# Softmax weights in PSUM, one sum of each unit on GpSimd, and shared PSUM banks in a fused local-attention and mixer kernel

## The chip, the cores and the metric

The kernel runs on one core of a Trainium2 chip. A core has five engines that work beside each other, each through its own queue in order: TensorE (PE, matmuls; PEld is its weight loads), VectorE (DVE), ScalarE (ACT), GpSimd (POOL) and SyncE (SP), which here issues all DMA transfers. SBUF is the working memory; PSUM, where matmuls put their results, has eight banks of 128 x 512 fp32. The metric is device time in microseconds (us), the median of several runs.

## The reference

For x of 2048 tokens by 512 channels:

```python
xn = layernorm(x)
q, k, v = split(xn @ wqkv)           # 32 heads of 16
# each position looks at itself and 7 earlier ones, 2 apart
logits = einsum(q, k[pos - 2 * r]) * 16 ** -0.5      # r = 0..7, masked before the start
s = (einsum(softmax(logits), v[pos - 2 * r])) @ wo
y = layernorm(xn)
g = silu(gelu(y @ w1 + b1) @ w2 + b2)                # 512 -> 1376 -> 512
out = x + s * g
```

## The kernel before, in words

Tokens are laid out as 128 partitions by 16; with a dilation of 2 the even and the odd tokens are two independent halves (c = 0, 1) of 8 tiles each. Attention is cut into 8 *units*, numbered u: (c = 0, 1) x (4 groups of 8 heads). Matrix products are made in fp16 with the operands split into a high and a low half, three matmuls for one.

For a unit, `qkv` makes 8 tiles of q, k, v with 12 matmuls of 384 columns each (L632); ScalarE evacuates each tile to the buffer `U` (L648), of which there are two, and DMAs make the shifted copies of k and v at the partitions' edges (`HALO`, L657). `attention` then works on DVE: four products of q with two shifts of k each (L691), each followed by a reduction over the 16 channels of a head (L694), the softmax over 8 positions (L714 to L721, with the exponential on ScalarE, L717), four products of the weights with two shifts of v each (`pv`, L747), and sums of these. The products are 128 x 2048 fp32 and live in the ring `R_prod` of three buffers. In units 0 to 6 DVE adds the second and third product to the first (`addto`, L742); what is left, three half-wide sums, is done on GpSimd during the next unit (`beside`, L771), each behind a one-element copy (L770) that makes it start when a certain product of DVE is done, so that it runs while DVE reduces. Unit 7 has no next one and sums on DVE. `emit_o` scales and splits the result (ScalarE L730, DVE L732) and a DMA transposes it into `oT` (L735).

The mixer's two layers are 4 chunks (`ch`) of 512 tokens, each with 11 steps f. `mlp1` makes 12 matmuls of 512 columns (L900), then ScalarE applies gelu in place (L917) and writes the high half h (L920). The low half is made in one of two ways, chosen by `DVE_LO`: DVE subtracts (L923), or PE subtracts h by a matmul with a negative diagonal (L929) and ScalarE writes the rest (L932). Steps 0 to 7 of the first chunk take the second way. `mlp2` (L945) adds 12 matmuls into four banks `z`, two steps later. After 11 steps ScalarE evacuates these with silu (L961, L956). The output projection `wo` (L817) runs for the first half of the tokens in `wo_first`, and at the end for the second half in `wo_last`, where the matmuls of the last unit's heads come last.

PSUM before: two banks `ps` (attention's tiles, wo), two banks `mh` (first layer), four banks `z`.

The order on every engine is not written out by hand. Each operation is entered in a plan with an engine, an estimated duration, a priority and its reads and writes; `issue` places them one after the other, always the one that can start first and among these the most urgent, and gives out ring buffers and banks as they come free in the plan. `port=True` tells the plan that a DVE and a GpSimd operation may not run beside each other. A change of a duration, a ring or a flag therefore reorders all queues. On the chip, every engine runs its list in the order planned and waits on semaphores.

The subtraction, as an example of an entry (L922 to L925): it is entered with the urgency of the first layer, ahead of attention's products, but in its queue it waits for the instruction before it like any other.

Of the kernel before, what the change touches and what calls it, by code (L numbers as in the profile page):

```python
# [8 lines left out]
F32 = mybir.dt.float32  # L9
# [4 lines left out]
ALU = mybir.AluOpType  # L14
# [4 lines left out]
P = 128  # L19
# [31 lines left out]

BEFORE_W1 = (0, 1, 4, 5)

DVE_LO = range(8, 44)


class Buf:
# [233 lines left out]
def tile_mixer(ctx, tc, a_x, a_wqkv, a_wo, b_w1, b_b1, b_w2, out):  # L291
# [18 lines left out]
    def dve(n, fn, r, w, f=1.0, port=True, c=0.065, **k):  # L310
        pl.add("dve", c + n * DVE1 * f, fn, r, w, port=port, **k)
# [45 lines left out]
    R_s = Ring(sb, [P, 8], F32, 10, "s")  # L357
    R_w = Ring(sb, [P, 16], F32, 8, "lw")
    R_bn = Ring(sb, [P, 6], F32, 4, "bn")
    R_ps = Ring(psum, [P, 512], F32, 2, "ps")  # L360
    R_mh = Ring(psum, [P, 512], F32, 2, "mh")
    R_z = [Ring(psum, [P, 512], F32, 1, f"z{i}") for i in range(4)]

    def f32v(t, k):
# [246 lines left out]
    def qkv(c, hb, u):  # L611
        ub = u % 2
        U3 = U[ub].rearrange("p (s e) -> p s e", e=P)
        cs = R_cs.new()
        act(NI, lambda: nc.scalar.activation(cs.t, cT[:, c], AF.Identity, scale=qsc[:, hb, 1:2]),
            [("c", c, i) for i in range(NI)] + [("qi", hb)], [cs], prio=PEV) if u else [
            dve(len(g), lambda q=cpos[g[0]], n=len(g), g=g: nc.vector.tensor_scalar(
                cs.t[:, q:q + n], cT[:, c, q:q + n], 1.0 / YS if g[0] in FP else qsc[:, hb, 1:2], None, op0=ALU.mult),
                [("c", c, i) for i in g] + ([] if g[0] in FP else [("qi", hb)]), [(cs, g)], prio=0.15)
            for g in groups]  # L620
        cp = lambda i: cpos[i] if c == 0 else i
        csk = {i: (cs, g) for g in groups for i in g} if u == 0 else {i: cs for i in range(NI)}
        for n, i in enumerate(IORD if u else IORD0):
            more = n % 2 and (u == 0 or u == 1 and n < U1MH)
            y = yT[c * 2 + i // 4]
            o = (i % 4) * P
            b = (R_mh if more else R_ps).new()

            def mm(n0=0, n1=12, y=y, o=o, b=b):
                for n in range(n0, n1):  # L630
                    (s, t), k = ((0, 0), (1, 0), (0, 1))[n // KT], n % KT
                    nc.tensor.matmul(b.t[:, 0:384], y[:, s, k, o:o + P], wq[:, hb, t, k],  # L632
                                     start=(n == 0), stop=(n == 11))

            ends = [4, 8, 12] if u < 2 else [12]
            if u == 0 and i in FP:
                yf = yF[i]
                for k in range(KT):
                    pe(1, 384, lambda k=k, b=b, yf=yf: nc.tensor.matmul(
                        b.t[:, 0:384], yf.t[:, k * P:(k + 1) * P], stq[hb]()[:, k * 384:(k + 1) * 384],  # L640
                        start=(k == 0), stop=(k == KT - 1)), [yf, ("stq", hb, k)], [b], fp32=4.1,
                       holds=stkey[hb], after=pl.users([b] + [("v", ub, i)]))
                ends = []
            for n0, n1 in zip([0] + ends, ends):
                pe(n1 - n0, 384, lambda mm=mm, n0=n0, n1=n1: mm(n0, n1), [("yh" if n1 <= 4 else "y", c, i)] +
                   [("wq" if n1 == 12 else "wqh", hb, k) for k in range(min(n1, KT))], [b],
                   after=pl.users([b] + [("v", ub, i)]))
            act(384, lambda i=i, b=b: nc.scalar.activation(  # L648
                U3[:, i:i + 31:15, :], b.t[:, 0:384].rearrange("p (t e) -> p t e", t=3),
                AF.Identity, scale=cs.t[:, cp(i):cp(i) + 1]), [b, csk[i], ("kz", ub)],  # L650
                [("q", ub, i), ("k", ub, i), ("v", ub, i)], prio=PEV)

        ks = [("k", ub, i) for i in range(1, 8)]
        vs = [("v", ub, i) for i in range(1, 8)]
        for x, h, o, src in (("k", KH, KO, ks), ("v", VH, VO, vs)):
            for n, (a, b) in enumerate(HALO):
                dma((b - a) * 3584, lambda a=a, b=b, h=h, o=o: nc.sync.dma_start(  # L657
                    U3[a:b, h:h + 7, :], U3[a - 1:b - 1, o + 1:o + 8, :]), src,
                    [(x + "h", ub, n)], rate=300e3, issue=0.6)
        vrow = v0[0:1, hb * P:(hb + 1) * P]  # L660
        if c == 0:
            dma(512, lambda: nc.sync.dma_start(vrow, U3[0:1, VO, :]), [("v", ub, 0)], [("v0", hb)])
        dma(3584, lambda: nc.sync.dma_start(
            U3[0:1, VH:VH + 7, :],
            vrow.rearrange("p (o e) -> p o e", o=1).to_broadcast([1, 7, P])),
            [("v0", hb), ("kz", ub)], [("vh0", ub)])
# [9 lines left out]
    def attention(c, hb, u):  # L676
# [35 lines left out]
        def over_r(t):  # L712
# [5 lines left out]
            table="exp", prio=PEV)  # L718
        dve(512, lambda: nc.vector.tensor_reduce(sx.t, Lt(), AX.X, ALU.add), Lk, [sx], port=False)
        dve(64, lambda: nc.vector.reciprocal(sx.t, sx.t), [sx], [sx], f=6.0, port=False)  # L720
        dve(512, lambda: nc.vector.tensor_tensor(Lt(), Lt(), over_r(sx.t), op=ALU.mult),  # L721
            [sx] + Lk, Lk)

        o16 = R_o.new()

# [18 lines left out]
        if u < 7:  # L744
            def pv(g):
                pr = R_prod.new()
                dve(2048, lambda: nc.vector.tensor_tensor(  # L747
                    pr.t.rearrange("p (r f d) -> p r f d", r=2, d=DH),
                    L3()[:, 2 * g:2 * g + 2].rearrange("p r (f o) -> p r f o", o=1)
                    .to_broadcast([P, 2, 64, DH]),  # L750
                    slots(Ut, VH, 2 * g).rearrange("p r (f d) -> p r f d", d=DH), op=ALU.mult),
                    Lk + vk + [("vh", ub, 0), ("vh", ub, 1), ("vh0", ub)], [pr])
                return pr

            def addto(a, b):
                add(2048, lambda: a.t, lambda: b.t, lambda: a.t, [a, b], a)
            acc = pv(0)
            p1 = pv(1)
            p2 = pv(2)
            addto(acc, p1)  # L760
            p3 = pv(3)
            addto(acc, p2)
            last.append(p3)

            def beside(x, y):
                def go(pr, p=PR_U * (u + 1) + 500):
                    def fn():
                        nc.gpsimd.tensor_copy(gate, pr.t[0:1, 0:1])  # L770
                        nc.gpsimd.tensor_tensor(x.t[:, 0:1024], x.t[:, 0:1024], y(), op=ALU.add)  # L771
                    pool(2.45, fn, [acc, p3, pr], [x, ("gate",)], prio=p)
                return go

            def rest(p=PR_U * (u + 2) + 700):
                with prio(p):
                    emit_o(lambda: acc.t[:, 0:1024], [acc], 0, 2)
            pend.extend([beside(acc, lambda: acc.t[:, 1024:2048]),
                         beside(p3, lambda: p3.t[:, 1024:2048]),
                         beside(acc, lambda: p3.t[:, 0:1024]), rest])  # L780
        else:

            for h in range(2):
                m = []
                for g in range(2):
                    pr = R_prod.new()
                    b0 = Ut[:, (VH + 4 * g + 4 * h) * P:]
                    win = bass.AP(b0.tensor, b0.offset, [list(b0.ap[0]), [P, 4], [DH, 32], [1, DH]])
                    dve(2048, lambda pr=pr, g=g, h=h, win=win: nc.vector.tensor_tensor(
                        pr.t.rearrange("p (r f d) -> p r f d", r=4, d=DH),  # L790
                        L3()[:, 4 * g:4 * g + 4, 32 * h:32 * h + 32]
                        .rearrange("p r (f o) -> p r f o", o=1).to_broadcast([P, 4, 32, DH]),
                        win, op=ALU.mult), Lk + vk + [("vh", ub, 0), ("vh", ub, 1), ("vh0", ub)], [pr])
                    m.append(pr)
                x, y = m
                for n, q0, q1 in ((2048, x, y), (1024, x, x), (512, x, x)):
                    add(n, lambda n=n, x=x: x.t[:, 0:n],
                        (lambda y=y: y.t) if n == 2048 else (lambda n=n, x=x: x.t[:, n:2 * n]),
                        lambda n=n, x=x: x.t[:, 0:n], [x] + ([y] if n == 2048 else []), x)
                emit_o(lambda x=x: x.t[:, 0:512], [x], h, h + 1)  # L800
# [36 lines left out]
    gu = [U[0][:, i * D:(i + 1) * D] for i in range(NI)]  # L837

    def wo_last():
        rings = [R_ps, R_ps, R_mh, R_mh] + R_z  # L840
        tiles = []
        for i in range(NI):
            b = rings[i].new()
            pe(9, 512, wo_mm(b, i, range(NHB - 1), NHB - 1 if i < NI - 1 else NHB - 2), [("oT", hb, i // 4) for hb in range(NHB - 1)] +
               [("wo", k) for k in (0, 2)], [b], prio=PR_M * 10 + 2 * i)
            tiles.append(b)
        for i in range(4):
            dma(P * 2048, lambda i=i: nc.sync.dma_start(gu[i], gd[1, i]),
# [389 lines left out]
```

## Time and profile before

| | us |
|---|---|
| median of 3 runs (423.68 to 424.52) | 423.83 |
| span of the profiled execution, first to last instruction | 422.0 |
| PE busy | 411.2 (97%) |
| DVE busy | 392.2 (93%) |
| ACT busy | 216.7 (51%) |
| POOL busy | 82.7 (20%) |

The profile gives the span of the one execution that was profiled, and not its whole time; the median of the runs stands 1.83 us above that span. The page has the busy time of each engine, the span in 40 slices with the busy share in tenths, and the chain of work that ended last. Groups give a line, an engine, an operation, the shapes and the count, then total busy time and the mean in ns of one, then the idle time ahead of them. Timelines give start and length in us. Matmul durations overlap, since matmuls are pipelined; their pace is read from the chain or from the distance of starts.

### The profile page before, as it was taken

The page shows a single profiled execution, that of the slowest core. Times are in us where ns is not written, and L with a number is a line of the kernel's source. Part 1 is how long each engine was busy: PE and PEld are TensorE (multiplying, and loading weights), DVE is VectorE, ACT ScalarE, POOL GpSimd, SP SyncE. Part 2 cuts the span into 40 slices and gives each one's busy share as a digit, 9 for nine tenths or more (in the row PEclk, how much of TensorE's full clock was granted, in tenths as well). Part 3 has the DMA queues.
Part 4 walks back from the last instruction along what each step waited for, and adds up shares of the span by engine and source line. Part 5 has one row for each costly group of instructions (what it writes and reads, how often), then busy time and mean ns, then how long its engine had stood idle before and what let it go on. Part 6 is the DMA issues. An engine that isn't in the chain of part 4 may idle for free.

```text
span 422.0 us, 5549 instructions
## 1 busy us (share of the span) xinstructions
PE 411.2 (97%) x2103; PEld 210.2 (50%) x2103; DVE 392.2 (93%) x402; ACT 216.7 (51%) x327; POOL 82.7 (20%) x119
## 2 busy tenths in 40 slices
PE   7899999999999899999999999999999999999995
PEld 5466544445644454445544554455545554444442
DVE  5958999999999999999999999998999989999974
ACT  6799983953367355854375352234230492236400
POOL 5310200002322341102500240052002500250022
PEclk8999999999999999999999999999999999999999
DMA  8962250310164036544252023110425374007142
GB/s 295 412 233 88 82 205 2 102 49 0 30 159 149 4 90 123 125 99 52 84 153 100 2 86 50 52 64 37 136 75 176 75 217 146 2 0 204 52 135 107
DMA packets 42650, 44.83 MB, mean 106 GB/s; under 512 B 27480, under 2 KB 27920, under 8 KB 42112
## 3 DMA queue, kind: packets, MB, share of 16 engines
q1 hardware_dynamic: 42624, 44.49, 35.4%
q8 instruction: 16, 0.26, 0.3%
q14 instruction: 10, 0.08, 0.1%
HBM read 23.53 MB, written 7.34 MB: 73 GB/s over the span
## 4 chain that ended last, share of the span: by engine, by line
PE 78%; DVE 15%; ACT 2%; issue 2%; POOL 1%; DMA 1%; SPq 0%; DVEq 0%
PE z L945 23%; PE ps L632 22%; PE mh L900 22%; PE ps L817 6%; DVE w L437 2%; PE z L817 2%; DVE prod L691 2%; DVE L L694 2%; PE mh L632 1%; DVE bn L525 1%; PE mh L817 1%; POOL cT L519 1%; DMA prod<-in_A_x_dram 1%; DVE prod L747 1%; DVE prod L742 1%
## 5 line engine op out<-in xcount | busy, mean ns | idle before, releaser
L900 PE MATMUL mh<-yT,w 128*128 128x512 f16 (+1 forms) x528 | 121.3, 379 | 0.7 <-ACT h L932 0.6
L632 PE MATMUL ps<-wq,yT 128*128 128x384 f16 x684 | 115.4, 326 | 2.6 <-ACT U L648 1.6
L945 PE MATMUL z<-w,h 128*128 128x512 f16 x480 | 111.2, 379 | 0.0
L632 PEld LDWEIGHTS <-yT 128*128 128x128 f16 x744 | 72.7, 98 | 51.6 <-issue 1.8
L900 PEld LDWEIGHTS <-w 128*128 128x128 f16 (+1 forms) x528 | 52.9, 100 | 61.8 <-issue 1.3
L917 ACT ACTIVATE mh<-mh,b1T,hsc 128x512 f32<-128x512 f32 (+1 forms) x44 | 33.0, 749 | 89.0 <-PE mh L900 88.6
L945 PEld LDWEIGHTS <-h 128*128 128x128 f16 x480 | 47.0, 98 | 55.0
L691 DVE TENSOR_TENSOR prod<-U 128x2048 f32<-128x2048 f32 x32 | 73.0, 2287 | 1.3 <-DMA U<-U 0.5
L694 DVE TENSOR_REDUCE L<-prod 128x128 f32<-128x2048 f32 x32 | 72.8, 2281 | 0.3
L648 ACT ACTIVATE U<-ps,cs 128x384 f32<-128x384 f32 x58 | 33.4, 577 | 60.9 <-PE ps L632 58.7
L747 DVE TENSOR_TENSOR prod<-L,U 128x2048 f32<-128x2048 f32 x28 | 63.1, 2285 | 0.2
L770 POOL COPY gate<-prod 1x1 f32<-1x1 f32 x21 | 4.4, 210 | 222.4 <-DVE prod L691 190.6
L742 DVE TENSOR_TENSOR prod<-prod,prod 128x2048 f32<-128x2048 f32 x16 | 36.5, 2282 | 0.0
L771 POOL TENSOR_TENSOR prod<-prod 128x1024 f32<-128x1024 f32 x14 | 32.9, 2349 | 0.0
L817 PEld LDWEIGHTS <-oT 128*128 128x128 f16 x189 | 18.5, 98 | 22.2
L920 ACT ACTIVATE h<-mh,hsc 128x512 f16<-128x512 f32 x40 | 27.4, 684 | 0.9
L817 PE MATMUL ps<-wo,oT 128*128 128x512 f16 x120 | 27.2, 379 | 0.0
L923 DVE SCALAR_TENSOR_TENSOR h<-mh,hsc,h 128x512 f16<-128x512 f32 x32 | 23.7, 741 | 0.9 <-ACT h L920 0.9
L730 ACT ACTIVATE o<-prod,osc 128x1024 f16<-128x1024 f32 (+1 forms) x9 | 9.4, 1050 | 14.4 <-POOL prod L771 8.9
L771 POOL TENSOR_TENSOR prod<-prod,prod 128x1024 f32<-128x1024 f32 x7 | 16.4, 2348 | 0.0
L917 ACT ACT_TABLE_LOAD x10 | 12.8, 1283 | 0.2
L810 POOL TENSOR_TENSOR U<-U,f 128x512 f32<-128x512 f32 x4 | 5.1, 1273 | 34.1 <-DVE U L880 34.1
(159 smaller groups left out, 363.6 us busy)
## 6 DMA issues: line engine op xcount, KB each, us to landing
f<-in_A_x_dram SPq DMA_DIRECT2D x31, 256.0 KB, 3.4
U<-U SPq DMA_DIRECT2D x16, 392.0 KB, 4.1
gd<-f SPq DMA_DIRECT2D x12, 256.0 KB, 2.6
oT<-in_B_w_dram SPq DMA_DIRECT2D x2, 1024.0 KB
yT<-in_B_w_dram SPq DMA_DIRECT2D x2, 1024.0 KB, 13.1
f<-gd SPq DMA_DIRECT2D x8, 256.0 KB, 2.9
out_dram<-f SPq DMA_DIRECT2D x8, 256.0 KB, 2.1
out_dram<-U SPq DMA_DIRECT2D x7, 256.0 KB, 2.0
```

Of the source, the lines that this page charges most:

```text
L632: nc.tensor.matmul(b.t[:, 0:384], y[:, s, k, o:o + P], wq[:, hb, t, k], start=(n == 0), stop=(n == 11))
L648: act(384, lambda i=i, b=b: nc.scalar.activation(U3[:, i:i + 31:15, :], b.t[:, 0:384].rearrange("p (t e) -> p t e", t=3), AF.Identity, sca ...
L691: dve(2048, lambda p2=p2, g=g: nc.vector.tensor_tensor(p2(), q, slots(Ut, KH, 2 * g), op=ALU.mult), qk + [("kh", ub, 0), ("kh", ub, 1), (" ...
L694: dve(2048, lambda pr=pr, g=g: nc.vector.tensor_reduce(L3()[:, 2 * g:2 * g + 2], pr.t.rearrange("p (r f d) -> p r f d", r=2, d=DH), AX.X, ...
L742: dve(n, lambda: nc.vector.tensor_tensor(d(), a(), b(), op=ALU.add), keys, [dkey])
L747: dve(2048, lambda: nc.vector.tensor_tensor(pr.t.rearrange("p (r f d) -> p r f d", r=2, d=DH), L3()[:, 2 * g:2 * g + 2].rearrange("p r (f ...
L771: nc.gpsimd.tensor_tensor(x.t[:, 0:1024], x.t[:, 0:1024], y(), op=ALU.add)
L817: nc.tensor.matmul(b.t, oT[:, hb, i // 4, s, i % 4], wo[:, t, hb], start=(hb == 0 and n == 0), stop=(hb == last and n == 2))
L900: nc.tensor.matmul(b.t[0:M], w1[:, s, k, f * P:f * P + M], yT[ch][:, t, k], start=(n == 0), stop=(n == 11))
L917: act(512, lambda: nc.scalar.activation(b.t[0:M], b.t[0:M], AF.Gelu_apprx_tanh, bias=b1T[0:M, f:f + 1], scale=hsc[0:M, 1:2]), [b, ("b1T",) ...
L920: act(512, lambda: nc.scalar.activation(hi()[0:M], b.t[0:M], AF.Identity, scale=hsc[0:M, 2:3]), [b], [hk])
L945: nc.tensor.matmul(z.t, hl[s][0:K, t * P:(t + 1) * P], w2[0:K, w, f], start=(f == 0 and n == 0), stop=(f == NF - 1 and n == 2))
```

## The change

Four things are changed.

1. The normalised softmax weights are written to a PSUM bank `A` instead of back to `L`, and the four products with v read them there. They are entered with `port=False`.
2. In units 0 to 6 GpSimd adds the second product to the first (a sum of 128 x 2048, entered with 4.75 us), DVE adds the fourth to the third, and the three half-wide sums on GpSimd follow as before. `R_prod` still has three buffers.
3. `ps` and `mh` become one ring of three banks; the fourth bank is `pl`, which holds A, some tiles of the first two `qkv`, and one tile of `wo_last`.
4. `DVE_LO` covers all 44 steps: the low half is always subtracted by DVE.

```diff
-DVE_LO = range(8, 44)
+DVE_LO = range(0, 44)
...
-    R_ps = Ring(psum, [P, 512], F32, 2, "ps")
-    R_mh = Ring(psum, [P, 512], F32, 2, "mh")
+    R_ps = R_mh = Ring(psum, [P, 512], F32, 3, "ps")
+    R_pl = Ring(psum, [P, 512], F32, 1, "pl")
...
-            more = n % 2 and (u == 0 or u == 1 and n < U1MH)
+            more = n % 4 == 3 and (u == 0 or u == 1 and n < U1MH)
...
-            b = (R_mh if more else R_ps).new()
+            b = (R_pl if more else R_ps).new()
...
-        dve(512, lambda: nc.vector.tensor_tensor(Lt(), Lt(), over_r(sx.t), op=ALU.mult),
-            [sx] + Lk, Lk)
+        A = R_pl.new()
+        A3 = lambda: A.t.rearrange("p (f r) -> p r f", r=W)
+        dve(512, lambda: nc.vector.tensor_tensor(A.t.rearrange("p (f r) -> p f r", r=W), Lt(), over_r(sx.t),
+                                                 op=ALU.mult), [sx] + Lk, [A, ("A", u)])
...
-                    L3()[:, 2 * g:2 * g + 2].rearrange("p r (f o) -> p r f o", o=1)
+                    A3()[:, 2 * g:2 * g + 2].rearrange("p r (f o) -> p r f o", o=1)
...
-                    Lk + vk + [("vh", ub, 0), ("vh", ub, 1), ("vh0", ub)], [pr])
+                    [A] + vk + [("vh", ub, 0), ("vh", ub, 1), ("vh0", ub)], [pr], port=False)
...
-            def addto(a, b):
-                add(2048, lambda: a.t, lambda: b.t, lambda: a.t, [a, b], a)
             acc = pv(0)
             p1 = pv(1)
+            pool(4.75, lambda: nc.gpsimd.tensor_tensor(acc.t, acc.t, p1.t, op=ALU.add), [acc, p1], [acc])
             p2 = pv(2)
-            addto(acc, p1)
             p3 = pv(3)
-            addto(acc, p2)
-            last.append(p3)
+            add(2048, lambda: p2.t, lambda: p3.t, lambda: p2.t, [p2, p3], p2)
+            last.append(p2)
...
-            pend.extend([beside(acc, lambda: acc.t[:, 1024:2048]),
-                         beside(p3, lambda: p3.t[:, 1024:2048]),
-                         beside(acc, lambda: p3.t[:, 0:1024]), rest])
+            pend.extend([beside(acc, lambda: acc.t[:, 1024:2048]),
+                         beside(p2, lambda: p2.t[:, 1024:2048]),
+                         beside(acc, lambda: p2.t[:, 0:1024]), rest])
...
-        rings = [R_ps, R_ps, R_mh, R_mh] + R_z
+        rings = [R_ps, R_ps, R_ps, R_pl] + R_z
...
-               [("wo", k) for k in (0, 2)], [b], prio=PR_M * 10 + 2 * i)
+               [("wo", k) for k in (0, 2)] + [("A", 7)] * (rings[i] is R_pl), [b], prio=PR_M * 10 + 2 * i)
```

The four products of unit 7 read A in the same way. The new sum and the last sum become lines 759 and 744 of the changed kernel, the products 749 and 787, the subtraction 921; other lines move by two.

More of the change, by code (lines that the diff above doesn't have):

```diff
@@ L771, in fn @@
                         nc.gpsimd.tensor_tensor(x.t[:, 0:1024], x.t[:, 0:1024], y(), op=ALU.add)
-                    pool(2.45, fn, [acc, p3, pr], [x, ("gate",)], prio=p)
+                    pool(2.45, fn, [acc, p2, pr], [x, ("gate",)], prio=p)
                 return go
@@ L790, in attention @@
                         pr.t.rearrange("p (r f d) -> p r f d", r=4, d=DH),
-                        L3()[:, 4 * g:4 * g + 4, 32 * h:32 * h + 32]
+                        A3()[:, 4 * g:4 * g + 4, 32 * h:32 * h + 32]
                         .rearrange("p r (f o) -> p r f o", o=1).to_broadcast([P, 4, 32, DH]),
-                        win, op=ALU.mult), Lk + vk + [("vh", ub, 0), ("vh", ub, 1), ("vh0", ub)], [pr])
+                        win, op=ALU.mult), [A] + vk + [("vh", ub, 0), ("vh", ub, 1), ("vh0", ub)], [pr], port=False)
                     m.append(pr)
```

## The prediction

> **What bounds the kernel now.** I read the page's busy times and slices first, then the chain that ended last, then the busy times of two stretches.
>
> ```profile
> span 422.0 us, 5549 instructions
> PE 411.2 (97%) x2103; PEld 210.2 (50%) x2103; DVE 392.2 (93%) x402; ACT 216.7 (51%) x327; POOL 82.7 (20%) x119
> PE   7899999999999899999999999999999999999995
> DVE  5958999999999999999999999998999989999974
> PE 78%; DVE 15%; ACT 2%; issue 2%; POOL 1%; DMA 1%; SPq 0%; DVEq 0%
> ```
>
> ```profile
> 48.90:165.00 116.10, 113.81 (x581) 57.16 (x580) 113.85 (x112) 68.65 (x109) 21.32 (x30) 1.00 0.29 88
> 165.00:405.00 240.00, 240.00 (x1208) 119.05 (x1207) 232.56 (x174) 106.26 (x145) 42.85 (x62) 1.00 0.33 89
> ```
>
> TensorE (PE) holds the chain. From 165 to 405 us it is busy 240.00 of 240.00 us at granted clock 1.00; VectorE (DVE) follows with 232.56, so it is 7.4 us from being the bound. Only two things can shorten the run: less work on PE, or fewer of the holes that PE has before 165. The timeline of PE, then three rows of the chain in order of time, show the price of its work and the two holes worth naming:
>
> ```profile
> 79.68 2.75 PE L945 MATMUL z<-w,h 128*128 128x512 f16 x12
> 83.00 2.75 PE L900 MATMUL mh<-yT,w 128*128 128x512 f16 x12 [0.57 <-ACT h L932]
> 138.16 7.96 PE L632 MATMUL ps<-wq,yT 128*128 128x384 f16 x48
> 147.72 2.60 PE L632 MATMUL ps<-wq,yT 128*128 128x384 f16 x15 [1.59 <-ACT U L648]
> ```
>
> ```profile
> 101.36 13.65 PE ps L632 x84
> 115.01 2.59 PE mh L900 x12
> 142.67 3.63 POOL cT L519
> ```
>
> Twelve 512-column matmuls take 2.59 us on the chain, 0.216 each; a 384-column one takes 13.65/84 = 0.163. So the first hole is 83.00 - (79.68 + 2.59) = 0.73 us, and the second 147.72 - (138.16 + 48 x 0.163) = 1.76.
>
> **The change part by part.** Unit prices, from the groups by shape:
>
> ```profile
> L929 PE MATMUL mh<-h,dg 128*128 128x512 f16 x8 | 3.0, 378 | 0.0
> L917 ACT ACTIVATE mh<-mh,b1T,hsc 128x512 f32<-128x512 f32 (+1 forms) x44 | 33.0, 749 | 89.0 <-PE mh L900 88.6
> L920 ACT ACTIVATE h<-mh,hsc 128x512 f16<-128x512 f32 x40 | 27.4, 684 | 0.9
> L923 DVE SCALAR_TENSOR_TENSOR h<-mh,hsc,h 128x512 f16<-128x512 f32 x32 | 23.7, 741 | 0.9 <-ACT h L920 0.9
> L437 DVE SCALAR_TENSOR_TENSOR w<-f,zsc,w 128x512 f16<-128x512 f32 (+1 forms) x3 | 2.1, 744 | 0.0
> L747 DVE TENSOR_TENSOR prod<-L,U 128x2048 f32<-128x2048 f32 x28 | 63.1, 2285 | 0.2
> L742 DVE TENSOR_TENSOR prod<-prod,prod 128x2048 f32<-128x2048 f32 x16 | 36.5, 2282 | 0.0
> L771 POOL TENSOR_TENSOR prod<-prod 128x1024 f32<-128x1024 f32 x14 | 32.9, 2349 | 0.0
> L810 POOL TENSOR_TENSOR U<-U,f 128x512 f32<-128x512 f32 x4 | 5.1, 1273 | 34.1 <-DVE U L880 34.1
> ```
>
> Back to back a DVE product or sum costs about 2.20 us (the rows' durations overlap by 0.08), a low-half subtraction 0.66.
>
> *No subtractions on PE.* Eight L929 matmuls go: 8 x 0.216 = 1.73 us off the bound engine. The first hole goes too, because PE waited there for ScalarE's L932, which no longer exists: 0.73. Eight subtractions move to DVE: 8 x 0.66 = 5.3 us, each behind whatever DVE is doing, at 54 to 105 us, where DVE has no idle time. What that costs PE I follow below.
>
> *Sums on GpSimd.* Seven DVE sums go: 7 x 2.20 = 15.4 us. From the two POOL rows, (2349 - 1273)/512 = 2.10 ns an element, so 2048 elements take 2349 + 1024 x 2.10 = 4.50 us. There are still three product buffers, so the fourth product waits until that sum frees the second. In the issue order of the changed kernel there stands between: one product (2.20) and one to three subtractions, with an output sum in two units. The holes left on DVE are 1.6 us in units 3 and 6, 1.0 in units 2 and 4, 0.3 in unit 1, none in 0 and 5: 5.5 us. DVE's net is 5.3 + 5.5 - 15.4 = -4.6 us. That is worth nothing by itself, since PE is the bound; it pays for the end (below).
>
> *Weights in PSUM.* Products now read one operand from PSUM. Subtractions with a PSUM operand (741) and an SBUF one (744) cost the same, so I take zero; dearer by 10%, 32 products would be 7 us on DVE. Writing PSUM may cost what ScalarE's two rows differ by (749 against 684, the first writes PSUM): 0.07 for each of 8 normalisations. Whether this frees GpSimd decides the 4.50 us:
>
> ```profile
> 125.93 3.68 POOL L512 TENSOR_TENSOR lw<-lw,halves 128x8 f32<-128x8 f32 x1 [7.35 <-DVE lw L504]
> 125.81 2.29 DVE L747 TENSOR_TENSOR prod<-L,U 128x2048 f32<-128x2048 f32 x1
> 281.26 0.57 POOL L770 COPY gate<-prod 1x1 f32<-1x1 f32 x1 [3.16 <-DVE prod L691]
> 281.11 0.68 DVE L808 TENSOR_TENSOR f<-f,f 128x512 f32<-128x512 f32 x1
> 365.00 0.17 POOL L770 COPY gate<-prod 1x1 f32<-1x1 f32 x1 [29.69 <-DVE prod L691]
> 364.78 0.75 DVE L923 SCALAR_TENSOR_TENSOR h<-mh,hsc,h 128x512 f16<-128x512 f32 x1
> ```
>
> The 8-wide power took 3.68 us: 2.17 until the SBUF-with-SBUF product ended at 128.10, then 1.51. The one-element copy took 0.57 beside such a sum and 0.17 beside a subtraction that reads PSUM. So GpSimd stands still beside DVE instructions with two SBUF inputs, and not beside those with one in PSUM. (The Trainium skill, "SBUF — State Buffer", Who interferes with whom, says that a VectorE tensor_tensor with both inputs in SBUF shuts out GpSimd's reads for its whole length; by that rule the new products leave it free, and the trace agrees.) I take 4.50; the other end, where each sum runs alone, is a rival.
>
> *Queues.* The fourth product's wait holds all of DVE's queue: the next subtraction, for which PE waits two steps later, and the next unit's first products. GpSimd's queue takes 7 x 4.50 us on 82.7 busy, and each sum stands ahead of the half sums of its own unit only. ScalarE loses 8 low halves and gains two table loads; at 51% it has room. SP's queue keeps its transfers but permutes those of the second layer norm (loads, gate stores, transposes) by a few places; I cost that at nothing because PE needs their result only at 192, and 2 us of slip there would show as the like wait on PE.
>
> *The second hole.* ScalarE's queue stood behind four scale instructions that waited for GpSimd's power (142.67, 3.63 us, held up by a product). In the changed order they stand fifteen instructions ahead of that unit's evacuations, and the product after the power reads PSUM: 1.76 gone. Next late are the low halves of the same stretch; the order leaves them 1 us or more before PE needs them.
>
> *Banks shared, and the subtractions in DVE's queue.* In the first MLP steps (call them f0, f1, ...) the changed order gives f3, f4 and f5 the same bank, so f4 waits until DVE has subtracted f3. Rows for it:
>
> ```profile
> 48.89 4.70 PE L900 MATMUL mh<-yT,w 128*128 128x512 f16 x21
> 49.18 4.84 DVE L437 SCALAR_TENSOR_TENSOR w<-yT,zsc,w 128x1024 f16<-128x1024 f32 x4
> 53.94 2.07 DVE L437 SCALAR_TENSOR_TENSOR w<-f,zsc,w 128x512 f16<-128x512 f32 x3
> 77.98 2.87 DVE L485 SCALAR_TENSOR_TENSOR wq<-yT,qsc,wq 128x768 f16<-128x768 f32 x3
> 85.26 1.06 ACT L383 ACTIVATE wo<-yT 128x1024 bf16<-128x1024 f32 x1 [0.90 <-DMA yT<-in_A_wo_dram]
> ```
>
> PE: f0 to f2 end at 48.89 + 3 x 2.59 = 56.7, second layer of f0 at 59.3, f3 at 61.8, second layer of f1 and four tiny sums at 65.0. DVE: four splits end at 54.0, then subtraction f0, three splits (2.0), f1, a product, f2, a reduction, a product, f3: 54.0 + 4 x 0.66 + 2.0 + 3 x 2.20 = 65.2. PE waits 0.3. By the same count f5 waits 0.1 at 72.5. Later PE has two sums over wo's squares ahead of f6's second layer. Those squares need wo loaded, and the load waits for the second L485 split: that ended at 79.8 and the squares began at 85.26, 5.4 later. DVE's three more subtractions put that split's end at 81.7, so squares begin at 87.4 behind ScalarE's f6 and f7 and end at 89.8; PE comes at 88.8: 1.2 with the hand-over. New waits: 1.6 us.
>
> *The end.* The order of the last projection changes: the oT half of the last unit is needed after 18 matmuls (3.9 us) instead of 36.
>
> ```profile
> 396.64 4.05 PE L817 MATMUL ps<-wo,oT 128*128 128x512 f16 x18
> 404.41 1.46 PE L817 MATMUL ps<-wo,oT 128*128 128x512 f16 x6
> 398.54 0.74 DVE L732 SCALAR_TENSOR_TENSOR o<-prod,osc,o 128x512 f16<-128x512 f32 x1
> DMA to landing us min/median/max: 3.1/4.5/6.1
> ```
>
> At present that half leaves DVE at 399.3 and lands 4.5 later, 403.8, for a need at 404.4. With PE 2.6 earlier the new need is 396.8 - 2.6 + 3.9 = 398.1, so DVE must be done by 393.6, 5.7 us earlier than now. It has 4.6 us less work and can lose part of its 7.4 idle, as the next unit's first product now stands where DVE waited for the exponential; following its order I get 390 to 391. I take no wait.
>
> **Sum.** Off: 1.73 + 0.73 + 1.76 = 4.2. On: 1.6. Net -2.6: the span becomes 419.4. The runs' median is 423.83, 1.83 above the profiled span (the profile gives no whole time of its own), so I forecast 421.2 us.
>
> **The rivals.**
> *DVE sets the end (slower).* One mechanism: the last unit's oT half is late and PE stands in the last projection. Each microsecond by which DVE leaves that half after 393.6 is one microsecond of PE; it loses to the kernel before from 396.2 on. If DVE gains nothing (399.3) the cost is 5.7 - 2.6 = 3.1: 426.9. If the PSUM operand doesn't free GpSimd, each of seven sums holds DVE 4.50 - 2.20 = 2.3 more than the sum it replaced: DVE has 16 + 5.3 us more than now against 7.4 idle, some 14 us late, 17 in all: 441. For it: DVE is at 99% after 165 and the holes are real. Against: the 0.17 copy. Chance 0.22, of which 0.05 for the lock.
> *The fill eats the gain (no change).* Subtractions have under 1.2 us of margin before DVE reaches them; one that is late holds DVE, whose queue holds the next. One product (2.20) more ahead of f3's subtraction is 2.2 more on PE: 423.4. Chance 0.13.
> *The new waits don't come:* -4.2, 419.6, inside the forecast's own range.
>
> **How the numbers follow.** Forecast 0.65, own range 419.6 to 423.0 (the new waits doubled). A change of 0.2%, 0.85 us, is about what this kernel's runs can tell. Faster: the forecast and a little of the second rival, 0.66; same: the rest of the second, 0.11; slower: 0.23. The 8-in-10 range reaches down to 419.4 and up to 426.9, DVE gaining nothing, and leaves out the lock and half of what lies between.
>
> **What would show it.** Right: no L929 and no wait on L932; GpSimd sums near 4.50 us beside products that stay at 2.29; no hole of PE near 147; PE waiting about a microsecond near 89 for the wo squares; PE solid from there to the end; DVE's last output half out before 394. Wrong: GpSimd sums or PSUM products that are longer; PE waits on L923's successor in 57 to 105; PE standing in the last projection for a DMA into oT; or new PE holes after 165 from three banks serving what four did.

## The result

The changed kernel takes 420.2 us (median of 4 runs, 419.93 to 421.31) where the kernel before takes 423.75 on the same chip: a ratio of 0.9918, 95% interval 0.9899 to 0.9938. The profiled span went from 422.0 to 418.2. Forecast were 421.2, with 419.4 to 426.9 as the range.

The page of the changed kernel, its busy times and PE's slices; below them the two stretches shown of the kernel before (length, then busy time of PE, PEld, DVE, ACT, POOL, granted clock, DMA share, GB/s):

```profile
span 418.2 us, 5558 instructions
PE 408.5 (98%) x2095; PEld 208.7 (50%) x2095; DVE 384.2 (92%) x403; ACT 214.8 (51%) x321; POOL 111.4 (27%) x126
PE   7799999999999999999999999999999999999995
```

```profile
48.90:165.00 116.10, 115.76 (x591) 58.16 (x589) 115.12 (x120) 67.20 (x106) 29.29 (x34) 1.00 0.31 90
165.00:405.00 240.00, 240.00 (x1209) 118.94 (x1207) 228.14 (x173) 105.53 (x142) 66.16 (x68) 1.00 0.33 93
```

By its busy time, which hides a pause shorter than the overlap of two matmuls, PE was idle before 165 us for 116.10 - 113.81 = 2.29 us and now is for 0.34. After 165 it was and is busy without a gap. DVE has 11.9 us of idle time there where it had 7.4. PE's timeline of the changed kernel at the places that the prediction named:

```profile
48.74 7.93 PE L898 MATMUL ps<-yT,w 128*128 128x512 f16 x36
...
63.06 2.10 PE L943 MATMUL z<-w,h 128*128 128x512 f16 x9
65.15 2.75 PE L898 MATMUL ps<-yT,w 128*128 128x512 f16 x12
67.74 4.70 PE L943 MATMUL z<-w,h 128*128 128x512 f16 x21
72.40 2.75 PE L898 MATMUL ps<-yT,w 128*128 128x512 f16 x12
...
88.59 0.28 PE L391 MATMUL ps<-s,fours 128*128 128x1 f32 x2
89.21 0.38 PE L391 MATMUL ps<-s,fours 128*128 128x1 f32 x2 [0.34 <-ACT wo L383]
89.45 2.75 PE L943 MATMUL z<-w,h 128*128 128x512 f16 x12
...
147.78 15.76 PE L632 MATMUL ps<-wq,yT 128*128 128x384 f16 x96
...
392.85 7.93 PE L815 MATMUL ps<-wo,oT 128*128 128x512 f16 x36
...
412.92 0.82 PE L865 MATMUL z<-wo,oT 128*128 128x256 f16 x6
```

Both holes of the kernel before, at 82.27 and 145.96, are gone. So is a third, shorter one that the prediction didn't name. In the kernel before, the last three matmuls of f1 and the first nine of f2 take 3.04 us from first start to last end instead of the usual 2.75 for twelve. f2 starts at 54.57, just after ScalarE has written the low half of f0:

```profile
53.63 3.04 PE L900 MATMUL mh<-yT,w 128*128 128x512 f16 x12
53.84 0.69 ACT L932 ACTIVATE h<-mh,hsc 128x512 f16<-128x512 f32 x1 [0.69 <-PE mh L929]
```

That hole is 0.29 us. What came on is small. f4 at 65.15 stands 0.15 us after the nine matmuls that begin at 63.06 (9 x 0.216 = 1.94), f5 at 72.40 stands 0.12 after the 21 that begin at 67.74, and the sums over wo's squares take 89.45 - 88.59 = 0.86 for 0.28 of work, a pause of 0.58. Together that is 0.85 us.

The groups that price the moved work (count, then total busy us and mean ns, then idle time before them):

```profile
L749 DVE TENSOR_TENSOR prod<-pl,U 128x2048 f32<-128x2048 f32 x28 | 63.2, 2281 | 4.3 <-POOL prod L759 4.2
L759 POOL TENSOR_TENSOR prod<-prod,prod 128x2048 f32<-128x2048 f32 x7 | 31.7, 4528 | 100.0 <-DVE prod L749 100.0
L602 DVE TENSOR_TENSOR f<-f,f 128x512 f16<-128x512 f32 x8 | 7.1, 884 | 0.0
L806 DVE TENSOR_TENSOR f<-f,f 128x512 f32<-128x512 f32 x8 | 6.5, 822 | 0.0
```

A GpSimd sum takes 4.53 us, and a product with a PSUM operand 2281 ns beside 2285 with both in SBUF. The last two groups, two-input sums of DVE that the change doesn't touch, are a surprise told of in the last section.

To compare runs I use one more number. Two profiles of the changed kernel differ in span (418.2 here, 419.1 in the run told of below as the changed kernel again) because the first MLP step f0 began at 48.74 in one and at 49.59 in the other. From f0's start to the start of PE's last group the two agree: 412.92 - 48.74 = 364.18 and 413.86 - 49.59 = 364.27. I call this PE's length; for the kernel before it is 416.71 - 48.89 = 367.82. What comes after that group (5.2 to 5.4 us in most runs) I call the tail.

### The profile page after: what moved, and what is told of

Same layout as the page of the kernel before. It is cut to its first block, busy times and chain, and to the rows that moved or that the text cites. A ratio compares the mean times of both kernels' runs of the same rounds, so it can differ in the third digit from the quotient of the medians.

```text
span 418.2 us, 5558 instructions
## 1 busy us (share of the span) xinstructions
PE 408.5 (98%) x2095; PEld 208.7 (50%) x2095; DVE 384.2 (92%) x403; ACT 214.8 (51%) x321; POOL 111.4 (27%) x126
## 4 chain that ended last, share of the span: by engine, by line
PE 81%; DVE 11%; ACT 4%; issue 1%; DMA 1%; SPq 0%; POOL 0%; DVEq 0%
PE ps L632 24%; PE z L943 24%; PE ps L898 22%; PE ps L815 7%; PE z L815 2%; DVE w L437 2%; DVE prod L691 2%; DVE L L694 2%; ACT w L436 1%; DMA prod<-in_A_x_dram 1%; DVE bn L525 1%; PE pl L632 1%; DVE h L921 1%; PE pl L815 1%; DVE w L434 1%
## 5 line engine op out<-in xcount | busy, mean ns | idle before, releaser
L898 PE MATMUL ps<-yT,w 128*128 128x512 f16 (+1 forms) x528 | 120.8, 379 | 0.0
L632 PE MATMUL ps<-wq,yT 128*128 128x384 f16 x708 | 117.9, 326 | 1.0 <-DVE yT L582 1.0
L915 ACT ACTIVATE ps<-ps,b1T,hsc 128x512 f32<-128x512 f32 (+1 forms) x44 | 32.8, 748 | 87.1 <-PE ps L898 86.9
L691 DVE TENSOR_TENSOR prod<-U 128x2048 f32<-128x2048 f32 x32 | 73.0, 2285 | 2.8 <-DMA U<-U 1.7
L648 ACT ACTIVATE U<-ps,cs 128x384 f32<-128x384 f32 x61 | 35.1, 578 | 65.1 <-PE ps L632 63.6
L749 DVE TENSOR_TENSOR prod<-pl,U 128x2048 f32<-128x2048 f32 x28 | 63.2, 2281 | 4.3 <-POOL prod L759 4.2
L759 POOL TENSOR_TENSOR prod<-prod,prod 128x2048 f32<-128x2048 f32 x7 | 31.7, 4528 | 100.0 <-DVE prod L749 100.0
L815 PE MATMUL ps<-wo,oT 128*128 128x512 f16 x132 | 29.6, 379 | 0.0
L921 DVE SCALAR_TENSOR_TENSOR h<-ps,hsc,h 128x512 f16<-128x512 f32 x40 | 29.5, 741 | 0.1
L918 ACT ACTIVATE h<-ps,hsc 128x512 f16<-128x512 f32 x40 | 27.2, 683 | 0.8
L744 DVE TENSOR_TENSOR prod<-prod,prod 128x2048 f32<-128x2048 f32 x9 | 20.5, 2278 | 0.0
## 6 DMA issues: line engine op xcount, KB each, us to landing
oT<-in_B_w_dram SPq DMA_DIRECT2D x2, 1024.0 KB, 11.9
```

The source lines that it names most:

```text
L648: act(384, lambda i=i, b=b: nc.scalar.activation(U3[:, i:i + 31:15, :], b.t[:, 0:384].rearrange("p (t e) -> p t e", t=3), AF.Identity, sca ...
L691: dve(2048, lambda p2=p2, g=g: nc.vector.tensor_tensor(p2(), q, slots(Ut, KH, 2 * g), op=ALU.mult), qk + [("kh", ub, 0), ("kh", ub, 1), (" ...
L749: dve(2048, lambda: nc.vector.tensor_tensor(pr.t.rearrange("p (r f d) -> p r f d", r=2, d=DH), A3()[:, 2 * g:2 * g + 2].rearrange("p r (f ...
L759: pool(4.75, lambda: nc.gpsimd.tensor_tensor(acc.t, acc.t, p1.t, op=ALU.add), [acc, p1], [acc])
L815: nc.tensor.matmul(b.t, oT[:, hb, i // 4, s, i % 4], wo[:, t, hb], start=(hb == 0 and n == 0), stop=(hb == last and n == 2))
L898: nc.tensor.matmul(b.t[0:M], w1[:, s, k, f * P:f * P + M], yT[ch][:, t, k], start=(n == 0), stop=(n == 11))
```

## The experiments

The prediction gives a sum with a reason for each term. The runs first take away one part of the change at a time, then make one part alone. Every edit is planned anew by the kernel's own planner, so a difference is that of the edit with the order it leads to, except where I say that the order is kept.

**The subtractions alone.**

```diff
 # the kernel before
-DVE_LO = range(8, 44)
+DVE_LO = range(0, 44)
```

> The kernel before with the eight subtractions on DVE and nothing else of the change (weights in SBUF, all sums on DVE, two pairs of banks). Theory: on PE eight matmuls (1.73 us) and the hole at 82.27 (0.73) go, the hole near 146 (1.76) stays, so 2.5 us are gained in front; but DVE has 5.3 us more and no relief, and the last unit's oT half, which left DVE at 399.3 for a need at 399.9, comes 2 to 5 us late: 422 to 426 in all, with a PE wait in the last projection. Rival, that the end doesn't hang on DVE: 421.3, no PE wait at the end.

Measured: 426.77 us, ratio 1.0061 (1.0048 to 1.0074); slower, and by more than the upper end. A row of PE's waits (total us, times, longest) and the second stretch:

```profile
PE mh L900 <- DVE h L923: 4.5, 4, 2.1
```

```profile
165.00:405.00 240.00, 236.56 (x1192) 117.39 (x1191) 233.25 (x172) 107.23 (x147) 43.08 (x62) 1.00 0.36 96
```

The loss comes in two places: steps of the first layer wait 4.5 us for a bank that DVE has still to read, which I had not counted, and the tail is 7.3 us long instead of 5.3, since DVE's output work is late. The wait of PE in the last projection that I expected isn't there. Nor did the hole near 146 stay: with the same two banks PE runs that QKV without a stop:

```profile
149.82 15.76 PE L632 MATMUL ps<-wq,yT 128*128 128x384 f16 x96
```

In this order ScalarE's scale instructions, at 157.12, wait only 0.67 us for the power. The hole at 82.27 is gone too, as expected.

**The change without the subtractions.**

```diff
 # the changed kernel
-DVE_LO = range(0, 44)
+DVE_LO = range(8, 44)
```

> The changed kernel with the eight subtractions back on TensorE. Theory: the eight matmuls cost 1.73 us again and the wait on ScalarE's low half up to 0.73, while the waits for the shared bank go (0.2): 420.2 + 1.7 to 2.4 = 421.9 to 422.6. Rival, that the gain comes from the freed GpSimd and the banks alone: 420.2 within 0.4.

Measured: 422.09, ratio 0.9948 (0.9934 to 0.9962). PE's length is 414.62 - 48.65 = 365.97, 1.79 more than with the subtractions on DVE, where eight matmuls are 1.73. So within the changed kernel this part is worth its matmuls, and the wait for ScalarE's low half, which I had added to it with 0.73, is not there.

**The change without the sums on GpSimd.**

```diff
 # the changed kernel
-            pool(4.75, lambda: nc.gpsimd.tensor_tensor(acc.t, acc.t, p1.t, op=ALU.add), [acc, p1], [acc])
+            add(2048, lambda: acc.t, lambda: p1.t, lambda: acc.t, [acc, p1], acc)
```

> The changed kernel with the seven 2048-wide sums back on DVE, weights still in PSUM. Theory: DVE gets 7 x 2.20 = 15.4 us back and loses 4.2 of waiting, so it runs out of its 11.9 us of idle time between 165 and 405, the last unit's oT half (391.7 at present, needed by 393.6) comes 2 to 7 us too late, PE stands in the last projection: 422 to 427. Rival, that the sums had cover enough and GpSimd's help is worth nothing: 420.2 within 0.4.

Measured: 424.06, ratio 0.9989 (0.9976 to 1.0001); nearly the whole gain is lost. The last unit's oT half on DVE's timeline (at 390.99 in the changed kernel):

```profile
404.46 0.74 DVE L734 SCALAR_TENSOR_TENSOR o<-prod,osc,o 128x512 f16<-128x512 f32 x1
```

The half is 13.5 us later. PE stands little, as the planner put other matmuls first (its length is 365.14), but the outputs that DVE makes from the last tiles pile up behind it: the tail is 8.2 us. So the loss stands where expected, at the end, though in DVE's output work more than in a pause of PE.

**The weights in SBUF.** PE and DVE execute the same instructions in the same order; only the place that the normalisation writes and the products read is another.

```diff
 # the changed kernel
-        A3 = lambda: A.t.rearrange("p (f r) -> p r f", r=W)
-        dve(512, lambda: nc.vector.tensor_tensor(A.t.rearrange("p (f r) -> p f r", r=W), Lt(), over_r(sx.t),
-                                                 op=ALU.mult), [sx] + Lk, [A, ("A", u)])
+        A3 = lambda: L.t.rearrange("p (f r) -> p r f", r=W)
+        dve(512, lambda: nc.vector.tensor_tensor(Lt(), Lt(), over_r(sx.t),
+                                                 op=ALU.mult), [sx] + Lk, Lk + [A, ("A", u)])
...
-                    [A] + vk + ...
+                    [A] + Lk + vk + ...
```

> The changed kernel with the normalised weights in SBUF in place of PSUM; each engine's instructions stand in the same order. Theory (GpSimd stands still beside a DVE instruction with two SBUF inputs): each GpSimd sum waits for the product beside it, 4.5 becomes 6.7, the fourth product starts 2.2 later in each of seven units, 15 us on DVE against 11.9 idle, the powers take 3.6 again and the hole near 146 comes back: 424 to 430. Rival, that the place of the weights doesn't matter: 420.2 within 0.4, sums at 4.53.

Measured: 431.01, ratio 1.0157 (1.0143 to 1.0171), a little above the upper end. The two groups, then one sum and the product beside it on the timeline, then the second power and the scale instructions that wait for it:

```profile
L749 DVE TENSOR_TENSOR prod<-L,U 128x2048 f32<-128x2048 f32 x28 | 70.8, 2553 | 9.9 <-POOL prod L759 9.8
L759 POOL TENSOR_TENSOR prod<-prod,prod 128x2048 f32<-128x2048 f32 x7 | 39.1, 5588 | 96.6 <-DVE prod L749 81.8 <-ACT h L918 14.8
```

```profile
187.42 4.51 POOL L759 TENSOR_TENSOR prod<-prod,prod 128x2048 f32<-128x2048 f32 x1 [16.54 <-DVE prod L749]
187.82 6.25 DVE L749 TENSOR_TENSOR prod<-L,U 128x2048 f32<-128x2048 f32 x1
229.52 6.41 POOL L759 TENSOR_TENSOR prod<-prod,prod 128x2048 f32<-128x2048 f32 x1 [14.81 <-DVE prod L749]
```

```profile
137.54 3.62 POOL L519 TENSOR_TENSOR cT<-lw,halves 128x8 f32<-128x8 f32 x1 [0.30 <-DVE lw L518]
141.19 0.87 ACT L615 ACTIVATE cs<-cT,qsc 128x8 f32<-128x8 f32 x4 [2.94 <-POOL cT L519]
```

Whichever comes second stands still. At 187.42 the sum was first: it ends at 191.93, and the product begun at 187.82 ends at 194.07, 2.14 later, about its own length (2.20 back to back). At 229.52 the product was first and the sum took 6.41 instead of 4.51. So GpSimd's sums and products with two SBUF inputs exclude each other, in both directions (the Trainium skill, "SBUF — State Buffer", Summary: rules for kernel authors, says that where a VectorE instruction has two SBUF inputs and the GpSimd one reads SBUF, the second to issue blocks fully until the first finishes; the trace agrees, with the 2.14 us above). Half of my expectation on the power fell, however: it takes 3.62 again, the scale instructions wait 2.94 for it, and yet the hole of 1.76 doesn't come back. The scale instructions end at 142.06, and the QKV begins at 148.64. (It has two shorter stops, 1.17 us together, but both go back to DVE: ScalarE's evacuation waits for a product, and a bank for a subtraction.) The product that reads PSUM was then not what removed the hole; the order or the banks were. Runs further down ask which. PE's idle time after f0 is 8.5 us in this run, nearly all of it ahead of the last projection.

**The changed kernel again**, as the measure of its group.

> The changed kernel itself, beside which the other runs of this group stand on one chip. All theories: 0.9918 of the kernel before, within its interval of 0.990 to 0.994.

Measured: 420.57, ratio 0.9909 (0.9896 to 0.9923). The two rows from which its PE's length is taken:

```profile
49.59 7.93 PE L898 MATMUL ps<-yT,w 128*128 128x512 f16 x36
...
413.86 0.82 PE L865 MATMUL z<-wo,oT 128*128 128x256 f16 x6
```

**One sum over wo's squares later.** Only PE's order differs, by the place of this sum, two one-column matmuls.

```diff
 # the changed kernel; the planner is told a longer time for the squares, so it places the sum later
-              lambda k=k: wo[:, 0, k:k + 2].rearrange("p k f -> p (k f)"), ("woh", k), 1024)
+              lambda k=k: wo[:, 0, k:k + 2].rearrange("p k f -> p (k f)"), ("woh", k), 1600)
```

> The changed kernel with one tiny matmul moved: the second sum over wo's squares stands on PE six second-layer matmuls (1.30 us) later; every other queue is the same. Theory, that PE's 0.5 us pause at 88.9 is that sum's wait for ScalarE's squares and nothing else stands behind it: the pause goes, PE ends 0.5 us earlier, 419.7 or 0.12% under the changed kernel. Rival, that f6's subtraction or wo's split is as late: the pause stays under another name, 420.2.

Measured: 419.98, ratio 0.9897 (0.9882 to 0.9912), 0.59 us under the changed kernel beside it, with intervals that overlap. The first stretch of this run:

```profile
48.90:165.00 116.10, 116.10 (x594) 58.32 (x593) 115.17 (x121) 68.08 (x106) 28.57 (x34) 1.00 0.31 89
```

By its busy time PE has no gap left, and its length is 413.06 - 49.45 = 363.61, 0.57 to 0.66 under the changed kernel's. The pause was that sum's wait and cost what it showed.

**The weights in PSUM, with the banks shared by three and one.**

```diff
 # the changed kernel
-DVE_LO = range(0, 44)
+DVE_LO = range(8, 44)
...
-            pool(4.75, lambda: nc.gpsimd.tensor_tensor(acc.t, acc.t, p1.t, op=ALU.add), [acc, p1], [acc])
+            add(2048, lambda: acc.t, lambda: p1.t, lambda: acc.t, [acc, p1], acc)
```

> Of the change only the weights in PSUM with the shared banks; subtractions on PE and all sums on DVE as before. Theory, that the hole near 146 comes from GpSimd's powers held up by a product with two SBUF inputs: the powers take 1.65 us, the hole goes, 1.76 us are gained in front, and DVE, which has no relief, gives up to 1.5 of it back at the end: 422.0 to 423.6. Rival, that the hole comes from ScalarE's queue alone: it stays, 424.0 to 424.5.

Measured: 424.45, ratio 1.0003 (0.9994 to 1.0011), no gain. My theory missed; its rival gave the right time for a wrong reason, since there is no hole near 146. It came back elsewhere, as two rows of PE's timeline show:

```profile
196.98 9.95 PE L632 MATMUL ps<-wq,yT 128*128 128x384 f16 x60 [0.88 <-DVE hlast L921]
...
274.01 2.11 PE L632 MATMUL ps<-wq,yT 128*128 128x384 f16 x12 [0.98 <-DVE f L829]
```

PE now waits for DVE, each time for a bank that DVE has still to read: first one with a low half to subtract, then one with a tile of the first output projection. PE's length is 368.30, 0.48 more than before.

**Shared banks alone.**

```diff
 # the kernel before
-    R_ps = Ring(psum, [P, 512], F32, 2, "ps")
-    R_mh = Ring(psum, [P, 512], F32, 2, "mh")
+    R_ps = R_mh = Ring(psum, [P, 512], F32, 4, "ps")
```

> The kernel before with its four banks in one ring for QKV and MLP and no other edit (weights in SBUF). Theory, that sharing banks has no price and no worth of its own: both holes of the kernel before stay within 0.5 us each, powers 3.6 us, 423.7 to 425.0 (ratio 0.998 to 1.002). Rival, that the freer banks are what removes the holes: 421 to 422.5.

Measured: 422.58, ratio 0.9959 (0.9947 to 0.9972). The rival is right and my theory falls: the freer banks, with the order they lead to, remove both holes. The first stretch, then PE and ScalarE where the first hole was (L928 and L931 are the matmul and the low half that the prediction calls L929 and L932):

```profile
48.90:165.00 116.10, 115.92 (x593) 58.20 (x591) 115.64 (x114) 68.95 (x107) 20.83 (x32) 1.00 0.26 80
```

```profile
79.85 0.38 PE L928 MATMUL ps<-h,dg 128*128 128x512 f16 x1
...
82.66 2.75 PE L899 MATMUL ps<-yT,w 128*128 128x512 f16 x12
...
80.55 0.67 ACT L931 ACTIVATE h<-ps,hsc 128x512 f16<-128x512 f32 x1
```

ScalarE still writes the low half, but the next step at 82.66 has another bank to go to and follows at the usual 2.59. For the second hole this run leaves two readings open: in its order the power takes 2.77 us, and ScalarE's scale instructions wait just 1.09 for it. The next run keeps the order.

**Four banks for one unit's QKV.** The queues are those of the kernel before, but for the banks that this unit's instructions name.

```diff
 # the kernel before
-            more = n % 2 and (u == 0 or u == 1 and n < U1MH)
+            more = n % 2 and (u in (0, 3) or u == 1 and n < U1MH)
```

> The kernel before, with every other QKV tile of the one unit that runs at 138 to 163 us put into a bank of the MLP's ring; the queues are the same but for the banks named in them. Theory, formed after the run with shared banks alone: the hole near 146 needs a QKV that has two banks only, with four it goes although the power still takes 3.6 us and the four scale instructions still wait: 1.76 us off, 422.6 (ratio 0.996). Rival, the one of the prediction: the late power makes the hole whatever the banks, 424.4 (ratio 1.000).

Measured: 423.93, ratio 0.9988 (0.9978 to 0.9999), between the two. GpSimd's power, ScalarE's scale instructions, and PE's first of the unit's tiles, what follows the last, and two later waits:

```profile
143.51 3.62 POOL L519 TENSOR_TENSOR cT<-lw,halves 128x8 f32<-128x8 f32 x1 [13.06 <-DVE lw L518]
147.17 0.87 ACT L615 ACTIVATE cs<-cT,qsc 128x8 f32<-128x8 f32 x4 [3.24 <-POOL cT L519]
```

```profile
139.25 2.11 PE L632 MATMUL ps<-wq,yT 128*128 128x384 f16 x12
...
154.84 2.75 PE L945 MATMUL z<-w,h 128*128 128x512 f16 x12
...
276.58 2.11 PE L632 MATMUL ps<-wq,yT 128*128 128x384 f16 x12 [0.34 <-DVE f L831]
...
287.95 4.22 PE L632 MATMUL ps<-wq,yT 128*128 128x384 f16 x25 [0.18 <-DVE f L831]
```

The late power and ScalarE's wait are all there, and PE does its 96 matmuls in 154.84 - 139.25 = 15.59 us without a stop. So the hole needed two things, the late power and a QKV with two banks only; here only the banks differ, and the hole goes. With the subtractions alone it went with the old two banks, where another order made the wait for the power short. But PE's length is 366.94, just 0.88 less than before: the other 0.9 was given back, nearly all at 276.58 and 287.95, where PE, being earlier, waits for a bank that DVE has still to read (its starts stand 0.51 and 0.34 us further apart there than its pace). That the hole costs 1.76 where it stands doesn't mean that removing it gains as much.

**Shared banks and the subtractions.**

```diff
 # the kernel before
-DVE_LO = range(8, 44)
+DVE_LO = range(0, 44)
...
-    R_ps = Ring(psum, [P, 512], F32, 2, "ps")
-    R_mh = Ring(psum, [P, 512], F32, 2, "mh")
+    R_ps = R_mh = Ring(psum, [P, 512], F32, 4, "ps")
```

> The kernel before with one ring of four banks and the eight subtractions on DVE; weights in SBUF, all sums on DVE. Theory, that the subtractions cost more at the end than they save on PE as long as DVE has no relief: 5.3 us more on DVE against 1.73 us less on PE, 424 to 426.5. Rival, that their loss without the rest of the change came only from MLP steps waiting for one of two banks: with four it goes and 1.73 us are gained on 422.6, 420.9.

Measured: 424.76, ratio 1.0013 (1.0003 to 1.0023). The first stretch and the last unit's oT half:

```profile
48.90:165.00 116.10, 116.10 (x592) 58.10 (x591) 115.13 (x118) 61.61 (x94) 18.98 (x25) 1.00 0.22 71
```

```profile
403.49 0.74 DVE L731 SCALAR_TENSOR_TENSOR o<-prod,osc,o 128x512 f16<-128x512 f32 x1
```

With four banks PE waits for no subtraction in front, and the kernel is still 2.2 us slower than with the banks alone: the half leaves DVE at 404.23, and the tail is 423.0 - 413.90 = 9.1 us. DVE sets the end, as the first rival of the prediction had it for a DVE without relief.

**One ring of four.** Here the weights take any free bank.

```diff
 # the changed kernel
-    R_ps = R_mh = Ring(psum, [P, 512], F32, 3, "ps")
-    R_pl = Ring(psum, [P, 512], F32, 1, "pl")
+    R_ps = R_mh = R_pl = Ring(psum, [P, 512], F32, 4, "ps")
...
-        rings = [R_ps, R_ps, R_ps, R_pl] + R_z
+        rings = [R_ps] * 4 + R_z
```

> The changed kernel with all four banks in one ring, the weights taking whichever is free, in place of three and one. Theory: PE has 0.85 us of waits left in the first MLP steps, of which the shared bank holds 0.3, so the most to be had is 0.3: 419.9 to 420.6 (ratio 0.990 to 0.991). Rival, that the weights now take a bank from the MLP when it is short of one, or wait for one with DVE behind them: 421 to 423.

Measured: 419.70, ratio 0.9896 (0.9881 to 0.9910), a little under the expected range. The first stretch:

```profile
48.90:165.00 116.10, 116.10 (x595) 58.51 (x594) 115.58 (x121) 68.39 (x107) 28.51 (x35) 1.00 0.30 89
```

PE's length is 413.08 - 49.67 = 363.41, 0.77 under the changed kernel: besides the bank waits the planner here also put the sum over wo's squares later. This is the fastest by the medians, level with the run that moved that sum alone; its interval overlaps the changed kernel's.

## Why the prediction was right, and where its reasons were not

| kernel | ratio to before | PE's length | tail |
|---|---|---|---|
| before | 1 | 367.82 | 5.3 |
| shared banks alone | 0.9959 | 366.29 | 5.3 |
| weights in PSUM (three banks and one) | 1.0003 | 368.30 | 5.2 |
| the same with the sums on GpSimd | 0.9948 | 365.97 | 5.4 |
| the same with the subtractions on DVE: the change | 0.9918, 0.9909 | 364.18, 364.27 | 5.3 |

*The sum.* Off 4.2, on 1.6, net -2.6, span 419.4, time 421.2. The trace has 4.2 off and 0.85 on, net -3.4, and PE's length fell by 3.64. The rest of 0.27 is the third hole, 0.29, which the prediction left out of its sum: it counted the holes "worth naming" at 2.49 where the trace has 2.78. The mechanism on PE was right. Mis-sized was the term "New waits: 1.6 us". Of its parts f4's 0.3 measured 0.15 and f5's 0.1 measured 0.12; the wait for wo's squares, put at 1.2, measured 0.58. The step that failed there: "squares begin at 87.4 behind ScalarE's f6 and f7 and end at 89.8". They stand where it says, but began at 86.96 and ended at 89.16, as ScalarE's timeline has it:

```profile
85.82 1.26 ACT L918 ACTIVATE h<-ps,hsc 128x512 f16<-128x512 f32 x2
...
86.96 1.07 ACT L383 ACTIVATE wo<-yT 128x1024 bf16<-128x1024 f32 x1
...
88.95 0.21 ACT L383 ACTIVATION_READ_ACCUMULATOR wo<-yT 128x1 f32 x1
```

Two slips of the working change nothing: the new waits doubled give 422.8 and not 423.0, and 396.8 should read 396.64.

*No subtractions on PE, 1.73 + 0.73.* The 1.73 was right to 0.06, measured at 1.79 by taking this part back. The 0.73 is not this part's: the hole "goes too, because PE waited there for ScalarE's L932, which no longer exists" is true of the trace, and with the subtractions alone the hole goes, as said; but with shared banks it goes while that instruction remains, so in the changed kernel this part adds nothing for it. Nor does the part pay by itself: alone it costs 0.6%, with shared banks more than the whole of their gain.

*The second hole, 1.76.* Its chain (late power, four scale instructions, ScalarE's queue) was read rightly, and in the changed kernel the power is early and short. But the given reasons, the order and "the product after the power reads PSUM", were one way of several. With the power at 3.62 and ScalarE waiting 2.94 the hole stays away, with four banks for this unit it goes in the old order, and with the two old banks it goes in another order. The condition that the prediction left out is that the QKV had two banks. That the holes then counted in full was partly luck: where this one alone was taken away, half of it came back as waits for DVE. In the changed kernel DVE has 11.9 us of idle time after 165, which probably is why it didn't; no run shows that by itself.

*Banks shared.* The prediction has this part only as a price, two waits. It is the part that removes both holes by itself, worth 1.8 us. With the weights in a bank of their own that is lost again (0.9959 to 1.0003), and the sums on GpSimd give it back (0.9948, an interval that overlaps that of shared banks alone). So weights and sums together gain nothing clear by themselves. They gain by what they let the subtractions do: 0.9918 with them, 1.0013 without.

*Sums on GpSimd.* 4.50 forecast, 4.53 measured. The holes of DVE behind them were put at 5.5 us and measured 4.2 in three waits, the longest 1.87. DVE's busy time was to fall by 15.4 - 5.3 = 10.1 and fell by 8.0. That this is "worth nothing by itself, since PE is the bound; it pays for the end" was right: without the sums the kernel is at 0.9989. Why DVE's fall was smaller the last section tells. The last unit's half, as the changed kernel has it,

```profile
390.99 0.74 DVE L734 SCALAR_TENSOR_TENSOR o<-prod,osc,o 128x512 f16<-128x512 f32 x1
```

leaves DVE at 391.73 where 390 to 391 were forecast, and PE doesn't stand in the last projection. The limit of 393.6 holds, but by luck. PE needs the half at 392.85 + 3.9 = 396.7 and not at 398.1, being earlier than forecast; and this transfer takes 3.1 us to land, in both kernels, where the prediction took 4.5, the median of all of them.

*Weights in PSUM.* Zero for the operand was right (2281 against 2285), and writing PSUM cost 0.01 us for each normalisation (697 ns against 688) where 0.07 was allowed. That it frees GpSimd was right and, in this order, is needed: 431.0 without it. An order planned for weights in SBUF wasn't run. The lock rival's 441 was too dear. It put 21 us more on DVE than before, which is 26 more than the forecast's -4.6; in the run DVE spent 7.6 us more on products and 5.6 more waiting for sums than the changed kernel does, 13.2 in all. Nor was its path the one that this run took, since PE's waits lay ahead of the last projection.

*The rivals.* That DVE sets the end didn't come in the changed kernel, where the half leaves DVE 1.9 us before the limit. It did come where the sums are taken back (0.9989) or the subtractions come without them (1.0013), in the tail and not as a stop of PE in the last projection. The fill ate 0.27 us, not 2.2.

## What to carry to other kernels

A hole that begins with a late engine may also need a ring that is too short to ride over it: before crediting an edit with the hole, ask whether one more bank would remove it, and test that alone. Edits that each lose or gain nothing (weights in PSUM, subtractions moved to the second busiest engine) can pay together once a third one has made room on that engine; price the set by the engine that would become the bound. And removing a hole gains what the next engine lets through: here 0.9 of 1.76 us, where PE then waited for DVE, which had 7.4 us to spare.

## What the runs showed of the hardware

GpSimd's sums and DVE's instructions with two SBUF inputs exclude each other (the lock of the prediction's first rival), and this costs DVE too. In the changed kernel two groups of sums with both inputs in SBUF take 884 and 822 ns each in the mean. The same groups of the kernel whose 2048-wide sums are back on DVE:

```profile
L602 DVE TENSOR_TENSOR f<-f,f 128x512 f16<-128x512 f32 x8 | 5.5, 702 | 0.4 <-ACT f L601 0.3
...
L806 DVE TENSOR_TENSOR f<-f,f 128x512 f32<-128x512 f32 x8 | 5.5, 681 | 0.0
```

The difference, 8 x 0.182 + 8 x 0.141 = 2.6 us, is of the size of what DVE's fall in busy time, 8.0, lacked of the forecast 10.1. Nearly all of it lies in three of the sixteen, those that began beside a 2048-wide sum of GpSimd. One of them, with that sum:

```profile
183.99 4.52 POOL L759 TENSOR_TENSOR prod<-prod,prod 128x2048 f32<-128x2048 f32 x1 [17.99 <-DVE prod L749]
187.26 1.81 DVE L602 TENSOR_TENSOR f<-f,f 128x512 f16<-128x512 f32 x1
```

GpSimd's sum ends at 188.51 and DVE's at 189.07, 0.56 later. The other two, at 144.09 and 265.85, take 0.99 and 1.81 us and end 0.55 and 0.54 after GpSimd's sum; the three are 0.31 + 1.13 + 1.13 = 2.57 us above 0.68. The products beside the same GpSimd sums, with one input in PSUM, keep 2281 ns. So in this kernel work given to GpSimd wasn't free for DVE: its sums with two SBUF inputs waited for the GpSimd sum beside them to end.
